# Attention and two expert layers on one core: 512-row groups in the second layer, 124-row blocks in the first

## Chip, cores and metric

The kernel runs on one core of a Trainium2 chip. The metric is the device time of one execution in microseconds. The profile shows one execution; "span" is the time from its first to its last instruction.

## What is computed

Attention with a block mask, then an expert layer that sends each of the 2304 tokens to two of eight experts, then one that sends each token to one of eight. Everything is in 32-bit floats. Cut from the reference:

```python
# q, k, v: 4 x 8 heads x 576 x 64; block mask of 64
scores = np.where(block_i >= block_j, scale * q @ k.T, -1e9)
x = softmax(scores) @ v                      # -> 2304 x 512
# first layer, w1: 8 x 512 x 1024, w2: 8 x 1024 x 512
noisy = x @ w_gate + np.log1p(np.exp(x @ w_noise)) * noise
top2 = the two largest of noisy, top2_w = their softmax
for e in range(8):
    h = np.maximum(x[mask] @ w1[e], 0.0)
    out[mask] += top2_w[mask, k, None] * (h @ w2[e])
# second layer, same shapes
logits = x @ w_gate2 + modality_bias[modality_id]
e_idx = argmax(logits); gate_w = softmax(logits)[e_idx]
out[mask] = gate_w[mask, None] * (np.maximum(x[mask] @ m2w1[e], 0.0) @ m2w2[e])
```

With these inputs the first layer's experts get 620, 582, 567, 546, 540, 559, 608 and 586 tokens. In the second layer experts 1 and 2 get 1165 and 1139 and the others none. Of the tokens that do not use expert 7 in the first layer, 866 and 852 go to these two.

## The kernel before

**Arithmetic.** Every 32-bit product is made of three matmuls in the faster 32-bit form: each operand is split into a high and a low part, and high x high, high x low and low x high are summed. For a weight piece of 128 x 1024, ScalarE copies `raw` to the high part `wh`, and VectorE or GpSimd subtracts to get the low part `wl` (`Stage.split`, L451). A job's weights are eight such pieces, fetched four ahead on SP's queue (`Stage.fetch`, L440).

**Jobs.** A `Job` (L466) is a set of rows for one expert. `gather` (L487) fetches its rows by index on GpSimd's queue into `xr`, `cols` (L499) transposes a block of 128 rows into PSUM `px` and splits it into `xth` (ScalarE) and `xtl` (VectorE). `mm1` (L511) is the first product, for each of eight column blocks of the hidden layer 12 matmuls over all rows of the job (in two halves where there are more than 512) into `ph`, evacuated to a high and a low part by ScalarE and VectorE (tiles `kp` and `hh`, `hl`). `mm2` (L527) is the second product, 24 matmuls of 512 columns for each block of 128 rows into `py`. The block's result `yr` is written by index: added to `X2` in the first layer, stored to the output in the second.

**Order of work.** The program is written out by a planner that keeps a clock for every engine (`clk`, L59) and emits each step when its estimated start is due; each engine then runs its instructions in the order written. `run` (L1407) goes through a list of jobs. During the second product of one job, `between` (L1428), called twice per block, puts in the transposes of the next job and the splits of its first four weight pieces; the other four are split during the first product, on the engines in the list `eb`.

**First layer.** Each expert has 640 places, five blocks of 128 (`CAP`, `NP`). Experts 0 and 1 begin with two and three blocks before attention has ended (`j00`, `j10`, tiles `ids0`), the rest of them follows (`j11`, `firsts[0]`), then experts 2 to 7. The routing runs in three steps (`route`, L650), for batches 0 and 1, batch 2, batch 3. Each turns the places of its tokens into lists: `hot_b` and `hot_a` make 0/1 operands `sl_ob`, `sl_oa` and `sl_ov`, and `lists` multiplies them on TensorE (`pt<-sl_ov,sl_ob`). `early` (L1135) makes from these the row numbers `idg` of a first job, which is gathered into the tile `wide`. Where more tokens choose an expert than it has places, a repair loop at the end of the program (L1593) runs.

**Notes.** For each finished block of the first layer eight dot products on VectorE (`zero<-py,gts,wide`) give the logits of the second layer, added by index to `LG`.

**Second layer.** `gates(k)` (L1466), the gate chain, reads `LG` back, picks each token's expert, counts with matmuls (`pt<-g_oh`), assigns tokens to groups of 256 rows, and makes the groups' lists in the same way. `gates(0)` starts after expert 6 and takes tokens that do not use expert 7: it fills three groups of 256 full rows (`NE`). `gates(1)` starts after expert 7 and fills seven (`NS`). The ten groups are jobs of two blocks (`group`, `job2`).

Of the kernel before, what the change touches and what calls it, by code (L numbers as in the profile page):

```python
# [7 lines left out]
F32 = mybir.dt.float32  # L8
# [22 lines left out]
def moe_kernel(tc, q, k, v, w_gate, w_noise, noise, w1, w2, mod_id, w_gate2, mod_bias, m2w1, m2w2, out):  # L31
# [6 lines left out]
    CAP = 640  # L38
    NP = CAP // 128

    FIRST = (2, 3)
    NE = 3
# [5 lines left out]
    NS = 10 - NE  # L48
# [55 lines left out]
    with ExitStack() as top:  # L104
# [18 lines left out]
        def iota(t, pattern, base=0, cm=0):  # L123
# [38 lines left out]
        table = [(cst.tile([128, 2 * n], I32, name="ids%d" % i), cst.tile([128, 2 * n], F32, name="gts%d" % i),  # L162
                  cst.tile([1, NG2 + 1], I32, name="eg%d" % i)) for i, n in ((2, NE), (3, NS), (4, NG2))]
# [25 lines left out]
        def consts2():  # L189
            iota(pad2, [[0, NA2]], base=NT + CAP, cm=1)  # L190
            iota(th2, [[G2, 9]])
            iota(th3, [[G2, 9]], base=G2 - 1)
            iota(th1, [[G2, 7]], base=CAP)
# [69 lines left out]
        def row_col(pool, pos, n):  # L263

            a = pool.tile([128, n], F32, name="sl_a%d" % n)
            bl = pool.tile([128, n], F32, name="sl_b%d" % n)
            vec.tensor_scalar(a, pos, 1.0 / 128, -63.5 / 128, op0=OP.mult, op1=OP.add)
            yield .3
            vec.tensor_scalar(a, a, 12582912.0, -12582912.0, op0=OP.add, op1=OP.add)
            yield .3  # L270
            vec.scalar_tensor_tensor(bl, a, -128.0, pos, op0=OP.mult, op1=OP.add)
            yield .3
            return a, bl
# [192 lines left out]
        class Job:  # L466


            def __init__(s, W, table, nt, ic, gc, emit, need=(None, None)):
# [29 lines left out]
            def cols(s, t, ps=None):  # L499
# [7 lines left out]
                cs = slice(128 * t, 128 * t + 128)  # L507
# [99 lines left out]
        def job1(e, t0=0, nt=NP, then=None, need=(None, None)):  # L607
            return Job((w1[e], w2[e]), X1, nt, lambda t: ids1[:, e * NP + t0 + t:e * NP + t0 + t + 1],
                       lambda t: gts1[:, e * NP + t0 + t:e * NP + t0 + t + 1], add_rows(ids1, e * NP + t0, nt, then), need)

        def group(W1, W2, table, ev, ic, gc, emit, need=(None, None)):
# [3 lines left out]
            return Job(w, table, G2 // 128, ic, gc, emit, need)  # L615
# [13 lines left out]
        def job2(k, g):  # L629
            ids, gts, eg = table[k]  # L630
            ic = lambda t: ids[:, 2 * g + t:2 * g + t + 1]
            j = group(m2w1, m2w2, X2, lambda: nc.sync.value_load(eg[0:1, g:g + 1], min_val=0, max_val=E - 1), ic,
                      lambda t: gts[:, 2 * g + t:2 * g + t + 1], put_rows(ic), ("eg%d" % k, "ids%d%d" % (k, g >= HG)))
# [12 lines left out]
        seconds = [job2(0, g) for g in range(NE)] + [job2(1, g) for g in range(NS)]  # L646
# [3 lines left out]
        def route(b0, nb):  # L650
# [81 lines left out]
            a, bl = yield from row_col(rt, pc.rearrange("p c k -> p (c k)"), 2 * C)  # L732
# [71 lines left out]
        with ExitStack() as ph:  # L804
# [330 lines left out]
            def early(e):  # L1135
# [11 lines left out]
                vec.tensor_scalar(base[:, e:e + 1], base[:, e:e + 1], 128.0 * n, None, op0=OP.max)  # L1147
# [259 lines left out]
        def run(jobs, hp_, ea, eb, nxt=None, stage=stage):  # L1407
# [3 lines left out]
            for n, j in enumerate(jobs):  # L1411
# [54 lines left out]
        def gates(k):  # L1466
# [4 lines left out]
            th = th2 if k else th3  # L1471
# [30 lines left out]
            n = yield from experts_of(pool, gn, gs, dst, "g_")  # L1502
            flags.add("eg%d" % k)
            if k == 1:

# [3 lines left out]
                no = yield from experts_of(pool, go, gso, eo, "o_")  # L1509
                m = pool.tile([1, 1], F32, name="g_m")  # L1510
                vec.tensor_scalar(m, n, -float(NS), 0.0, op0=OP.add, op1=OP.max)
                yield .3
                vec.tensor_add(m, m, no)
                yield .3
# [193 lines left out]
```

## Time and profile before

| | before |
|---|---|
| median of 3 runs | 992.0 us (990.72 to 994.84) |
| the profiled execution | 991.67 us |
| its span | 989.9 us |
| TensorE busy | 949.4 us (96%) |
| VectorE busy | 703.6 us (71%) |
| ScalarE, GpSimd busy | 520.9 and 521.0 us (53% each) |
| moved by DMA | 141.6 MB, mean 143 GB/s |
| mean granted TensorE clock | 0.993 of full speed |

Busy time is an average over stages. Attention runs up to about 268 us, the first layer to about 738 us, the second from there to the end. TensorE's matmuls overlap in the records, so the length of one matmul is not its price; the distance between starts is.

### The profile page before, as it was taken

What the parts mean: (1) busy time and instruction counts of PE and PEld (TensorE: products, weight loads), DVE (VectorE), ACT (ScalarE), POOL (GpSimd) and SP (SyncE); (2) the same over time, 40 slices, a digit from 0 to 9 for tenths busy, and PEclk for the clock granted to TensorE, in tenths of its full rate; (3) what the DMA queues carried; (4) which work ended last, traced back from release to release, by engine and by line L of the source; (5) the groups of instructions that cost most, each with busy time, mean ns of one, the idle gap of its engine ahead of it and who ended that gap; (6) DMA issues with size and microseconds to landing.
All of it is one profiled execution on the core that took longest, in us unless ns stands there. A gap on an engine that the chain in (4) does not pass through costs nothing.

```text
span 989.9 us, 17527 instructions
## 1 busy us (share of the span) xinstructions
PE 949.4 (96%) x6072; PEld 860.7 (87%) x6072; DVE 703.6 (71%) x1707; ACT 520.9 (53%) x1156; POOL 521.0 (53%) x488
## 2 busy tenths in 40 slices
PE   8999998999979999999999999999999899999995
PEld 6989897998868998989899898989979779999994
DVE  6878779888769967386693948669788866555450
ACT  6989997988542344334333333433335535555551
POOL 6234333464423599586685848648476253333321
PEclk9999999999989999999999999999999999999998
DMA  5577752222376377464563727434466877776620
GB/s 127 106 217 197 221 131 65 72 60 68 92 236 197 54 171 181 118 151 107 128 129 93 143 86 150 107 86 54 143 129 195 279 234 233 229 220 219 197 86 12
DMA packets 158258, 141.60 MB, mean 143 GB/s; under 512 B 76233, under 2 KB 124745, under 8 KB 158034
## 3 DMA queue, kind: packets, MB, share of 16 engines
q1 hardware_dynamic: 139042, 106.92, 37.4%
q0 software_dynamic: 18064, 33.23, 16.7%
q8 instruction: 50, 0.82, 0.3%
q14 instruction: 46, 0.38, 0.1%
q10 hardware_dynamic: 1056, 0.26, 0.1%
HBM read 112.54 MB, written 28.36 MB: 142 GB/s over the span
## 4 chain that ended last, share of the span: by engine, by line
PE 73%; DVE 9%; issue 5%; ACT 5%; DMA 4%; POOL 3%; SPq 1%; POOLq 0%; ACTq 0%; DVEq 0%
PE ph L71 28%; PE py L71 27%; PE pt L71 7%; PE ps L71 6%; PE pa L71 3%; PE px L71 2%; DVE wl L71 2%; ACT p L71 2%; POOL wl L71 2%; ACT kp L71 1%; DVE kp L71 1%; DMA xr<-X,ids 1%; DVE nm L71 1%; DVE PTl L71 1%; DMA qld<-in_q_dram 1%
## 5 line engine op out<-in xcount | busy, mean ns | idle before, releaser
L71 POOL TENSOR_TENSOR wl<-raw,wh 128x1024 fp32r<-128x1024 f32 x80 | 207.5, 2623 | 106.4 <-ACT wh L71 92.2
L71 PE MATMUL ph<-xth,wh 128*128 128x320 f32 (+2 forms) x800 | 241.2, 302 | 2.1 <-DVE kp L71 2.1
L71 PE MATMUL ph<-xth,wl 128*128 128x320 f32 (+2 forms) x800 | 240.0, 300 | 0.0
L71 PE MATMUL ph<-xtl,wh 128*128 128x320 f32 (+2 forms) x800 | 240.0, 300 | 0.0
L71 DVE SCALAR_TENSOR_TENSOR zero<-py,gts,wide 128x512 f32<-128x512 f32 x304 | 227.5, 748 | 8.3
L71 PE MATMUL py<-wh,kp 128*128 128x512 f32 x496 | 168.1, 399 | 0.0
L71 PEld LDWEIGHTS ph<-xth,wh 128*128 128x128 f32 x800 | 151.7, 190 | 4.0 <-DVE kp L71 2.8
L71 PEld LDWEIGHTS ph<-xtl,wh 128*128 128x128 f32 x800 | 151.7, 190 | 0.7
L71 PEld LDWEIGHTS ph<-xth,wl 128*128 128x128 f32 x800 | 151.7, 190 | 0.0
L71 ACT ACTIVATE wh<-raw 128x1024 fp32r<-128x1024 f32 x144 | 150.8, 1053 | 0.6 <-DMA raw<-in_moe_w_dram 0.5
L71 ACT ACTIVATE yr<-py,gts 128x512 f32<-128x512 f32 x60 | 41.3, 689 | 147.1 <-PE py L71 104.6
L71 PEld LDWEIGHTS py<-wh,kp 128*128 128x128 f32 x496 | 94.0, 189 | 18.5
L71 DVE SCALAR_TENSOR_TENSOR hl<-ph,hh 128x320 fp32r<-128x320 f32 (+2 forms) x100 | 46.4, 465 | 79.1 <-ACT hh L71 78.9
L71 DVE TENSOR_TENSOR wl<-raw,wh 128x1024 fp32r<-128x1024 f32 x64 | 80.1, 1259 | 29.8 <-ACT wh L71 29.1
L71 PE MATMUL py<-wl,kp 128*128 128x512 f32 x248 | 97.4, 393 | 0.0
L71 PE MATMUL ps<-kh,kp 128*128 128x256 f32 (+5 forms) x320 | 95.7, 340 | 0.6 <-ACT p L71 0.4
L71 POOL DMA_INDIRECT xr<-X,ids x55 | 57.5, 1045 | 73.5 <-PE px L71 44.2
L71 PE MATMUL py<-wh,hh 128*128 128x512 f32 x232 | 94.0, 405 | 0.0
L71 DVE TENSOR_TENSOR xtl<-px,xth 128x512 fp32r<-128x512 f32 x58 | 40.0, 690 | 74.3 <-ACT xth L71 74.3
L71 PE MATMUL py<-wl,hh 128*128 128x512 f32 x232 | 90.6, 390 | 1.7 <-POOL wl L71 1.7
L71 ACT ACTIVATE hh<-ph 128x320 fp32r<-128x320 f32 (+2 forms) x100 | 41.8, 418 | 95.1 <-PE ph L71 91.6
L71 PE MATMUL py<-wh,hl 128*128 128x512 f32 x232 | 90.9, 392 | 0.0
(253 smaller groups left out, 1830.9 us busy)
## 6 DMA issues: line engine op xcount, KB each, us to landing
raw<-in_moe_w_dram SPq DMA_DIRECT2D x144, 512.0 KB, 4.0
X<-zero SPq DMA_DIRECT2D x13, 512.0 KB, 4.2
kld<-in_k_dram SPq DMA_DIRECT2D x32, 128.0 KB, 2.9
vld<-in_v_dram SPq DMA_DIRECT2D x32, 128.0 KB, 2.7
X<-x SPq DMA_DIRECT2D x16, 256.0 KB, 2.6
qld<-in_q_dram SPq DMA_DIRECT2D x30, 128.0 KB, 2.8
wide<-in_moe_w_dram SPq DMA_DIRECT2D x4, 512.0 KB, 6.5
wide<-WG2T POOLq DMA_DIRECT2D x1, 2048.0 KB, 10.2
```

Source lines behind the costliest of these rows:

```text
L71: return f(*a, **kw)
```

## The change

**Second layer.** A group has 512 rows (`GW`), four blocks (`BW`). `gates(0)` fills two full groups, `gates(1)` two more full ones; what is left of each expert goes into two small groups, one of 256 rows and one of 128 (`job2(..., small=True)`, tile `egs`). In the group of 128 rows the first product reads its columns twice, so that each matmul has 256. With the inputs above this makes six groups out of ten: 512 rows of expert 1 and of expert 2, the same once more, then 141 tokens of expert 1 in 256 places and 115 of expert 2 in 128. `gates(1)` gets steps to assign the rest, and it now tells whether the repair loop must run by counting the placed tokens with one more matmul.

**First layer.** A block holds 124 tokens (`UNIT`), an expert 620 (`USED`). Neighbouring blocks overlap by four columns between the layers: the first product has 4 x 124 + 128 = 624 columns (two halves of 312) and the second reads blocks of 128 that begin at multiples of 124. The three-block job of expert 0 has 376 columns for 384. `j00`, `j10` and `j11` keep their steps of 128.

**Beside it.** In the second routing step `sl_ov` is made on VectorE instead of GpSimd (`b0 == 0`). For `firsts[0]` the four later weight pieces are split by GpSimd twice and then VectorE twice (`eb_`). The extra buffers for `raw` in the second layer are two instead of four.

```diff
+    UNIT = 124
+    USED = NP * UNIT
-    NE = 3
+    GW = 512
+    BW, NW, NSM = GW // 128, 2, 2
-    NS = 10 - NE
...
-        def row_col(pool, pos, n):
+        def row_col(pool, pos, n, u=128):
-            vec.tensor_scalar(a, pos, 1.0 / 128, -63.5 / 128, op0=OP.mult, op1=OP.add)
+            vec.tensor_scalar(a, pos, 1.0 / u, -(u - 1) / 2 / u, op0=OP.mult, op1=OP.add)
...
-                s.n = 128 * nt
+                s.n = step * (nt - 1) + 128
...
-                cs = slice(128 * t, 128 * t + 128)
+                cs = slice(s.step * t, s.step * t + (s.step if t < s.nt - 1 else 128))
+                pt = pt[:, :, 0:cs.stop - cs.start]
...
-                            ten.matmul(ph[:, 0:cn], w[:, kk], xx[:, kk, cs], start=(kk == 0 and i == 0), stop=(kk == 3 and i == 2))
+                            o, xx = ph[:, 0:cn], xx[:, kk, cs]
+                            if cn == 128:
+                                o, xx = ph[:, 0:2 * cn].rearrange("p (r c) -> p r c", r=2), bc(xx[:, None], [128, 2, cn])
+                            ten.matmul(o, w[:, kk], xx, start=(kk == 0 and i == 0), stop=(kk == 3 and i == 2))
...
-                cs = slice(128 * t, 128 * t + 128)
+                cs = slice(s.step * t, s.step * t + 128)
...
-        seconds = [job2(0, g) for g in range(NE)] + [job2(1, g) for g in range(NS)]
+        seconds = [job2(k, g) for k in range(2) for g in range(NW)] + [job2(1, g, True) for g in range(NSM)]
...
-                ov = yield from hot_a(rt, a[:, n], 10, 0, NA1, va[:, n], b0 + nb < B)
+                ov = yield from hot_a(rt, a[:, n], 10, 0, NA1, va[:, n], b0 == 0)
...
+                eb_ = [gps, gps, vec, vec] if j is firsts[0] else eb
-                        stage.split(eb[fs.index(f) % len(eb)] if "ids1" in flags else vec)
+                        stage.split(eb_[fs.index(f) % len(eb_)] if "ids1" in flags else vec)
...
             if k == 1:
+                nr = pool.tile([128, E], F32, name="g_nr")
+                vec.scalar_tensor_tensor(nr, gn, -float(GW), pp[:, NTT], op0=OP.mult, op1=OP.add)
+                gm, gr = yield from starts(pool, nr, th2, "q_")
+                yield from experts_of(pool, gm, gr, egs, "q_")
+                flags.add("egs")
...
+                    held = tl("held", dt=BF16)
+                    vec.tensor_copy(held, placed)
+                    pm = ps_r.tile([128, NTT], F32, name="pt")
+                    ten.matmul(pm, ones, held, start=True, stop=True)
+                    vec.tensor_reduce(m, pm[0:1], axis=AX, op=OP.add)
+                    vec.tensor_scalar(more, m, float(NT) - .5, None, op0=OP.is_lt)
...
-            with tc.tile_pool(name="ws2", bufs=4, reuse_waits="tile") as ws2:
-                rings["raw"].add(ws2, 4)
+            with tc.tile_pool(name="ws2", bufs=2, reuse_waits="tile") as ws2:
+                rings["raw"].add(ws2, 2)
```

**Where instructions move.** VectorE at the end of attention, before: the last weight halves and evacuation (`kp`) of the first job, then the routing's sum `acc` and the row numbers up to `idg`.

```order
L71 TENSOR_TENSOR wl<-qld,wh 128x512
L71 SCALAR_TENSOR_TENSOR kp_4115<-ps,kp_4115 128x256
L71 TENSOR_TENSOR acc_98<-acc_98,pt 128x200
L71 TENSOR_SCALAR si_u_4142<-acc_98 128x3
L71 SCALAR_TENSOR_TENSOR si_t_4141<-acc_98,pad_75 128x3
L71 SCALAR_TENSOR_TENSOR si_u_4142<-si_u_4142,acc_98 128x3
L71 TENSOR_TENSOR ids_101<-si_t_4141,si_u_4142 128x3
L71 TENSOR_TENSOR si_g_4147<-acc_98 128x3
L71 TENSOR_TENSOR gts_105<-si_g_4147,acc_98 128x3
L71 CAST i_4139<-ids_101 128x3
L71 TENSOR_SCALAR gp<-i_4139 128x3
L71 TENSOR_TENSOR idg_103<-gp,i_4139 128x3
```

VectorE at the same place after the change, from the list operands `sl_ov` on.

```order
L73 TENSOR_TENSOR sl_ov<-sl_oa,vals 128x1000 x2
L73 TENSOR_TENSOR wl<-kld,wh 128x512
L73 TENSOR_TENSOR wl<-qld,wh 128x512
L73 SCALAR_TENSOR_TENSOR kp_3955<-ps,kp_3955 128x256
L73 TENSOR_TENSOR acc_98<-acc_98,pt 128x200
L73 SCALAR_TENSOR_TENSOR kp_4039<-ps,kp_4039 128x256
L73 TENSOR_SCALAR si_u_4059<-acc_98 128x3
L73 SCALAR_TENSOR_TENSOR si_t_4058<-acc_98,pad_75 128x3
L73 SCALAR_TENSOR_TENSOR si_u_4059<-si_u_4059,acc_98 128x3
L73 TENSOR_TENSOR ids_101<-si_t_4058,si_u_4059 128x3
L73 TENSOR_TENSOR si_g_4064<-acc_98 128x3
L73 TENSOR_TENSOR gts_105<-si_g_4064,acc_98 128x3
```

`acc` stood behind all four pairs of weight halves and all eight evacuations; it now stands behind one pair and two evacuations. Between these rows and `idg` one more pair and one more evacuation follow. On TensorE the last seven of the ten list matmuls had all 96 matmuls of the first job's first product ahead of them; they now have 36 of them ahead and 60 behind.

TensorE at the start of the first group of the second layer, before: the last matmuls of expert 7's second product, then the group's first product.

```order
L71 MATMUL py<-wh,hh_8192 128x512
L71 MATMUL py<-wl,hh_8192 128x512
L71 MATMUL py<-wh,hl_8193 128x512
L71 MATMUL py<-wh,hh_8258 128x512
L71 MATMUL py<-wl,hh_8258 128x512
L71 MATMUL py<-wh,hl_8259 128x512
L71 MATMUL ph<-xth,wh 128x256
L71 MATMUL ph<-xtl,wh 128x256
L71 MATMUL ph<-xth,wl 128x256
```

TensorE at the same place after the change (`px` are the transposes of the group's rows).

```order
L73 MATMUL py<-wh,hh_8191 128x512
L73 MATMUL py<-wl,hh_8191 128x512
L73 MATMUL py<-wh,hl_8192 128x512
L73 MATMUL py<-wh,hh_8257 128x512
L73 MATMUL py<-wl,hh_8257 128x512
L73 MATMUL py<-wh,hl_8258 128x512
L73 MATMUL px<-ident,xr 128x128 x4
L73 MATMUL ph<-xth,wh 128x512
L73 MATMUL ph<-xtl,wh 128x512
L73 MATMUL ph<-xth,wl 128x512
```

The transposes of the fourth block stand immediately ahead of the first product, where twelve matmuls stood between them and the last transposes. Those of the second and third block stand twelve matmuls earlier, directly behind one another. One group later, the first transposes of the group whose rows `gates(1)` lists (`ids_110`) stand twelve matmuls behind the list matmuls, where they stood twenty-four behind.

## Rows read from the trace of the kernel before

**Rows 1.** The page, busy time of TensorE, with share of the span and instructions.
```profile
PE 949.4 (96%) x6072; PEld 860.7 (87%) x6072; DVE 703.6 (71%) x1707; ACT 520.9 (53%) x1156; POOL 521.0 (53%) x488
```
**Rows 2.** Waits of TensorE: line, waited for; us in total, times, longest.
```profile
PE px L71 <- DMA wide<-X,idg: 6.7, 1, 6.7
...
PE px L71 <- DMA xr<-X,ids: 3.1, 2, 1.9
PE ph L71 <- DVE kp L71: 2.1, 3, 1.1
PE py L71 <- POOL wl L71: 1.7, 1, 1.7
PE pt L71 <- DVE sl_ov L71: 1.6, 1, 1.6
```
**Rows 3.** Chain that ended last: start and length in us, what, instructions.
```profile
446.20 28.15 PE ph L71 x192
...
886.67 11.51 PE ph L71 x96
898.19 2.75 PE py L71 x12
901.37 2.77 PE py L71 x12
904.58 5.46 PE py L71 x24
```
**Rows 4.** Timeline, TensorE, 268 to 287 us: start, us, instruction, [idle before].
```profile
268.10 1.03 PE L71 MATMUL pt<-sl_ov,sl_ob 128*128 128x200 bf16 x10
...
278.58 1.11 PE L71 MATMUL px<-ident,wide 128*128 128x128 f32 x4 [6.67 <-DMA wide<-X,idg]
...
283.62 0.60 PE L71 MATMUL px<-ident,wide 128*128 128x128 f32 x4
...
286.82 0.60 PE L71 MATMUL px<-ident,wide 128*128 128x128 f32 x4
```
**Rows 5.** Timeline, GpSimd, 256 to 274 us.
```profile
256.34 4.42 POOL L71 TENSOR_TENSOR sl_ov<-sl_oa,vals 128x600 bf16<-128x600 bf16 x4
...
273.23 1.05 POOL L71 DMA_INDIRECT wide<-X,idg  x1 [9.78 <-DVE u L71]
```
**Rows 6.** Timeline, VectorE, 272 to 303 us.
```profile
272.31 0.16 DVE L71 TENSOR_TENSOR idg<-gp,i 128x3 int32<-128x3 f32 x1
...
302.33 1.20 DVE L71 TENSOR_TENSOR sl_ov<-sl_oa,vals 128x1000 bf16<-128x1000 bf16 x1
```
**Rows 7.** Stretches: busy PE, PEld, DVE, ACT, POOL; granted clock, DMA share, GB/s.
```profile
272.00:278.00 6.00, 0.00 (x0) 0.00 (x0) 1.46 (x8) 0.47 (x2) 2.95 (x3) 0.80 1.04 352
278.00:284.00 6.00, 5.42 (x21) 4.51 (x21) 3.10 (x9) 1.72 (x3) 0.00 (x0) 0.63 0.21 48
...
720.00:770.00 50.00, 47.04 (x296) 41.12 (x295) 44.42 (x107) 22.94 (x35) 34.35 (x22) 1.00 0.67 172
```
**Rows 8.** Timeline, GpSimd, 371 us: the late weight half of `firsts[0]`.
```profile
371.22 2.93 POOL L71 TENSOR_TENSOR wl<-raw,wh 128x1024 fp32r<-128x1024 f32 x1
```
**Rows 9.** Timeline, three engines, 726 to 733 us: the first group's rows.
```profile
726.58 1.02 POOL L71 DMA_INDIRECT xr<-X,ids  x1 [0.30 <-issue]
...
730.98 0.66 PE L71 MATMUL px<-ident,xr 128*128 128x128 f32 x4 [1.85 <-DMA xr<-X,ids]
...
731.47 0.95 POOL L71 DMA_INDIRECT xr<-X,ids  x1 [0.30 <-issue]
...
732.30 0.69 DVE L71 TENSOR_TENSOR xtl<-px,xth 128x512 fp32r<-128x512 f32 x1 [1.58 <-ACT xth L71]
```
**Rows 10.** Timeline, VectorE and TensorE, 803 to 810 us: the first late group's rows.
```profile
803.31 0.19 DVE L71 COPY g_acc<-pt 128x40 f32<-128x40 f32 x1
...
809.08 0.63 PE L71 MATMUL px<-ident,xr 128*128 128x128 f32 x4 [1.26 <-DMA xr<-X,ids]
```
**Rows 11.** The page, groups of instructions: busy us, mean ns of one, idle before.
```profile
L71 PEld LDWEIGHTS py<-wh,kp 128*128 128x128 f32 x496 | 94.0, 189 | 18.5
```

More of the change, by code (lines that the diff above doesn't have):

```diff
@@ L191, in consts2 @@
             iota(th2, [[G2, 9]])
-            iota(th3, [[G2, 9]], base=G2 - 1)
-            iota(th1, [[G2, 7]], base=CAP)
+            iota(th3, [[GW, 9]], base=GW - 1)
+            iota(th1, [[G2, 7]], base=USED)
             nc.sync.dma_start(wg2, w_gate2.rearrange("(k p) e -> p k e", p=128))
@@ L270, in row_col @@
             yield .3
-            vec.scalar_tensor_tensor(bl, a, -128.0, pos, op0=OP.mult, op1=OP.add)
+            vec.scalar_tensor_tensor(bl, a, -float(u), pos, op0=OP.mult, op1=OP.add)
             yield .3
@@ L466, in moe_kernel, with __init__ @@
         class Job:
-            def __init__(s, W, table, nt, ic, gc, emit, need=(None, None)):
+            def __init__(s, W, table, nt, ic, gc, emit, need=(None, None), step=128):
+                s.step = step
                 s.W, s.table, s.nt, s.ic, s.gc, s.emit, s.need = W, table, nt, ic, gc, emit, need
-                s.n = 128 * nt
+                s.n = step * (nt - 1) + 128
                 s.parts = [(0, s.n)] if s.n <= 512 else [(0, s.n // 2), (s.n // 2, s.n // 2)]
@@ L608, in job1, with group @@
             return Job((w1[e], w2[e]), X1, nt, lambda t: ids1[:, e * NP + t0 + t:e * NP + t0 + t + 1],
-                       lambda t: gts1[:, e * NP + t0 + t:e * NP + t0 + t + 1], add_rows(ids1, e * NP + t0, nt, then), need)
-        def group(W1, W2, table, ev, ic, gc, emit, need=(None, None)):
+                       lambda t: gts1[:, e * NP + t0 + t:e * NP + t0 + t + 1], add_rows(ids1, e * NP + t0, nt, then), need, 128 if nt == 2 else UNIT)
+        def group(W1, W2, table, ev, ic, gc, emit, need=(None, None), nt=G2 // 128):
             def w():
@@ L614, in w @@
                 return W1[bass.ds(e, 1)].rearrange("o d f -> (o d) f"), W2[bass.ds(e, 1)].rearrange("o f d -> (o f) d")
-            return Job(w, table, G2 // 128, ic, gc, emit, need)
+            return Job(w, table, nt, ic, gc, emit, need)
         prev_out = []
@@ L731, in route @@
             yield .3
-            a, bl = yield from row_col(rt, pc.rearrange("p c k -> p (c k)"), 2 * C)
+            a, bl = yield from row_col(rt, pc.rearrange("p c k -> p (c k)"), 2 * C, UNIT)
             big = rtile([128, 2 * C], "big")
@@ L1501, in gates @@
             gn, gs = yield from starts(pool, pp[:, NTT], th, "g_")
-            n = yield from experts_of(pool, gn, gs, dst, "g_")
+            yield from experts_of(pool, gn, gs, dst, "g_")
             flags.add("eg%d" % k)
             if k == 1:
+                nr = pool.tile([128, E], F32, name="g_nr")
+                vec.scalar_tensor_tensor(nr, gn, -float(GW), pp[:, NTT], op0=OP.mult, op1=OP.add)
+                yield .3
+                gm, gr = yield from starts(pool, nr, th2, "q_")
+                yield from experts_of(pool, gm, gr, egs, "q_")
+                flags.add("egs")
+                vec.tensor_scalar(gr, gr, 2.0, float(BW * NW), op0=OP.mult, op1=OP.add)
+                yield .3
+                vec.scalar_tensor_tensor(gr, gn, -float(BW), gr, op0=OP.mult, op1=OP.add)
+                yield .3
+                vec.tensor_add(nr, gs, gn)
+                yield .3
+                vec.tensor_scalar(nr, nr, NW + .5, 1e5, op0=OP.is_gt, op1=OP.mult)
+                yield .3
+                vec.tensor_add(gs, gs, nr)
+                yield .3
                 go, s_ = yield from starts(pool, base, th1, "o_")
@@ L1508, in gates @@
                 yield .3
[L1509 to L1514, printed above, removed]
-                vec.tensor_scalar(more, m, 1.0, None, op0=OP.min)
-                yield .3
+                yield from experts_of(pool, go, gso, eo, "o_")
             t0, pos, st = tl("t0", sh), tl("pos"), tl("st")
@@ L1602, in moe_kernel @@
             po = r1.tile(sh, F32, name="po")
-            vec.tensor_scalar(po, pos_k, float(CAP), 1e5, op0=OP.is_lt, op1=OP.mult)
-            vec.scalar_tensor_tensor(so, so, -float(CAP), po, op0=OP.add, op1=OP.add)
+            vec.tensor_scalar(po, pos_k, float(USED), 1e5, op0=OP.is_lt, op1=OP.mult)
+            vec.scalar_tensor_tensor(so, so, -float(USED), po, op0=OP.add, op1=OP.add)
             vec.tensor_copy(ovs.rearrange("p c k -> p k c"), so)
```

48 lines of the change are left out of this document (35 added, 13 removed).

## The prediction

> **What bounds the kernel now.** I read the busy times first: TensorE is busy for 949 us of the span [rows 1], far ahead of the others, so what counts is the time its instructions take and the moments when it stands still. The list of waits comes next [rows 2]: TensorE loses 6.7 us in one wait for a gather into `wide`, 3.1 us in two waits for gathered rows (1.85 and 1.26 us), 2.1 us in three for the evacuation `kp`, 1.7 us in one for a low weight half `wl` made on GpSimd, 1.6 us for `sl_ov`. The list has no others in the two layers' products. Then the chain of work that ended last [rows 3], which in these stretches is TensorE alone, gives the price of every matmul from one start to the next: 28.15 / 192 = 0.1466 us at 320 columns, 11.51 / 96 = 0.1199 at 256, 5.46 / 24 = 0.2275 at 512. From 256 to 512 columns that is 0.42 ns per column on top of a fixed 12 ns per matmul. Four transposes into `px` add 901.37 - 898.19 - 12 x 0.2275 = 0.45 us.
>
> **The change, part by part.** All sums are made against the profiled execution's own 991.67 us; the median of the runs, 992.0, is 0.3 above it.
>
> *Second layer, arithmetic.* I ran the reference on its inputs: only two experts are chosen in the second layer, 1165 and 1139 tokens. So ten groups of 256 rows become two groups of 512 early, two of 512 late, one of 256 and one of 128. First product: 960 matmuls x 0.1199 = 115.1 us before. Now 4 x 96 x 0.2275 = 87.4, plus 2 x 96 x 0.1199 = 23.0 (the 128-row group computes its columns twice, as 256): 110.4. Gain 4.7 us. Nothing in the trace has 512 columns in the first product; I take the price of the second product, which has the same number of columns and one weight load per matmul as well. Second product: 19 blocks instead of 20, 24 x 0.2275 = 5.5 us, and one set of transposes, 0.45. Sum 10.6 us, all of it on the path, since TensorE does not wait in these groups [rows 3].
>
> The Trainium skill (TensorE: Matmul & The Clock Gate, "Wait — 56ns, not 53.3ns?") gives a fixed cost of about 2.5 ns per matmul. By that, 384 matmuls fewer would save 1.0 us in the first product. The trace shows 12 ns [rows 3] and decides.
>
> *First layer, columns.* Six experts have 2 x 96 matmuls each with 312 columns for 320: 1152 x 8 x 0.42 ns = 3.9 us. The three-block part of expert 0 goes from 384 to 376: 0.3 us. Sum 4.2, on the path. The second product there still has 128 rows a block.
>
> *Weights.* 32 of 144 weight pieces are no longer loaded and split. TensorE hardly waits for them, so I count nothing for it; the cover is that a 512-row group lasts about 45 us where 256 rows last 23.4 [rows 3] for the same eight pieces. The 128-row group has the least cover, some 17 us, but its pieces are fetched ahead. Half the extra buffers in that phase (two for four) I also put at nothing.
>
> *End of attention.* Before, the list operands `sl_ov` of the second routing step are made on GpSimd in four operations, 4.42 us [rows 5], and the list matmuls stand behind all first-product matmuls of the first job, at 268.10 [rows 4]. The row numbers `idg` follow at 272.31 [rows 6], the gather is issued at 273.23 [rows 5], and TensorE, idle since 271.9, goes on at 278.58 [rows 4]. Now `sl_ov` takes two VectorE operations of 1.20 us [rows 6], in a stretch where VectorE waits for ScalarE between weight halves, and 60 matmuls that were ahead of the last list matmuls stand behind them: 60 x 0.12 = 7.2 us earlier. In VectorE's order two weight halves and two `kp` now stand between `acc` and `idg`, which gives back 1 to 2 us. So the gather starts 5.2 to 6.2 us earlier, at 267.0 to 268.0. It took 5.35 us [rows 4, 5] under full DMA load (352 GB/s in 272 to 278, [rows 7]); another took 4.4 us [rows 9]. It lands between 271.4 and 273.4, and TensorE asks at 271.9. I leave 0.5 us of the wait.
>
> After the wait the granted clock was 0.63 on average in 278 to 284, against 1.00 in 720 to 770 [rows 7], so part of the stretch ran at 1.2 GHz: transposes and 12 matmuls took 283.62 - 278.58 = 5.04 us where the next such set took 3.20 [rows 4]. These 1.84 us go with the wait. Gain 6.67 - 0.5 + 1.84 = 8.0 us. Next late there is nothing TensorE asks for: the weights of the second job were loading from 268 on.
>
> *Expert 0, rest.* TensorE waits 1.7 us [rows 2] for a `wl` that GpSimd made from 371.22 on, behind other work [rows 8]. Two of these four halves go to VectorE, which stands idle between evacuations there. Gain 1.7 us.
>
> *From the first layer to the second.* This part speaks against the change. Four blocks must be gathered and transposed where two were.
> - The first gather still makes TensorE wait about 1.85 us [rows 9].
> - Gathers follow each other by about 1.3 us on GpSimd; the third, issued at about 731.5, takes 4.4 like the first and lands near 735.9, while its transposes now stand directly behind the second block's, at about 735.0: 0.9 us.
> - The fourth block's transposes now stand immediately ahead of the first product. From the start of transposes to the end of `xtl` it is 732.30 + 0.69 - 730.98 = 2.0 us [rows 9], of which TensorE works 0.4: 1.6 us new.
> - The first late group's gather: its transposes wait until 809.08, 5.8 us after `acc` at 803.31 [rows 10], about 6.9 after the list matmuls. Between those and the transposes stood 24 matmuls, now 12 (2.7 us). The wait of 1.26 becomes 3.1 to 4.1; I take 3.5.
> - The other four waits of this stretch (`kp` twice, `g_oh`, `sl_ov`; 3.8 us in all, [rows 2] holds the sums) stem from the second gate chain, which gets some twenty short VectorE steps more (4 to 5 us), but about 9 us more of TensorE work to hide behind. Between 0 and 3.8; I take half, 1.9.
>
> Before: 1.85 + 1.26 + 3.8 = 6.9. After: 1.85 + 0.9 + 1.6 + 3.5 + 1.9 = 9.75. Loss 2.8 us. The tail behind the last matmul is unchanged.
>
> **Sum.** 10.6 + 4.2 + 8.0 + 1.7 - 2.8 = 21.7. 991.67 - 21.7 = 970.0; with the 0.3 up to the median, 970.3 us.
>
> **Rivals.**
> 1. *The passage to the second layer costs more.* The gate chain runs late in spite of the longer groups (3.8 instead of 1.9), the gather wait is 4.1, and one or two of the idle stretches bring the clock down. For it: the long idle stretch at 272 did so and cost 1.84 us; against it: 720 to 770, with 1.85 us of idle at 730.98, was granted 1.00 [rows 7, 9]. 970.3 + 1.9 + 0.6 + 2 x 1.84 = 976.5.
> The Trainium skill (the same page, "Why this matters for your kernels") warns that gaps between bursts of matmuls bring TensorE back to the low clock; that speaks for this rival, and rows 7 show it once.
> 2. *The longer groups hide the gate chain completely* and the fourth block costs little: 970.3 - 1.9 - 0.9 - 0.5 = 967.0.
> 3. *The gather at the end of attention stays late*, since the weight loads saturate the DMA at just that time: only 4 of the 8 us are won, 974.3.
> 4. *A first product at 512 columns costs just twice one at 256*: 4 x 96 x 2 x 0.1199 = 92.1 in place of 87.4 us, 4.7 less gain, 975.0. For it: no row has this form; against it: the prices at 256, 320 and 512 lie on one line [rows 3].
> The Trainium skill's 2.5 ns, named above, comes close to this case.
> 5. *Slower: weight loads from odd offsets.* Hidden blocks of the first layer now begin at multiples of 496 bytes and not 512. A weight load of 189 ns hides under a matmul of 227 [rows 3, 11]. Should the odd start cost it, 26 blocks x 24 loads are hit, and the gain is gone once a load takes more than 227 + 21.7 us / 624 = 262 ns; doubled (378 ns), it is 0.15 x 624 = 94 us, some 1064 us. Against it: the list matmuls read their moving operand in steps of 400 bytes, and ten of 200 columns took 1.03 us with their end [rows 4], no more than their columns need; for weights no row shows it.
> 6. *The change does not hold its rows.* By the reference the fullest first-layer expert has exactly 620 rows, and 5 x 124 = 620. One more, and the repair loop runs: at least one group of 23.4 us [rows 3] with nothing beside it, so 993.7 or more.
>
> **How the numbers follow.** Forecast 0.53, rival 1 0.17, rival 2 0.12, rivals 3 and 4 0.07 and 0.06, rivals 5 and 6 0.03 and 0.02. The forecast's own spread is about 4 us either way (the second-layer waits between their bounds, the gather between 0 and 1.5 us late). The range from 964.5 to 977 takes in rivals 1 to 4 and leaves out the two slow ones and mixtures of several misfortunes. About 0.5% is what a measurement of this kernel can tell from no change, 987 to 997 us: only a large part of rival 1, 3 and 5 together would end there, 0.02. Slower 0.04, faster 0.94.
>
> **What would show it.** After the change, the wait for the gather into `wide` should be under 1.5 us and the granted clock there 1.0; a 312-column expert should take 27.5 us in the first product and a 512-row one 21.8; the wait for `wl` near 365 us should be gone; and the waits on gathered rows should add up to some 6 us in place of 3.1, the largest ahead of the first late group, with a wait of `ph` on `xtl` new. Wrong would be: weight loads well over 189 ns in the first layer, a second or longer wait at the end of attention, or a gate chain that makes TensorE wait for more than 4 us.

## The result, and the profile after

The changed kernel takes 983.2 us (median of four runs, 979.6 to 984.6), 0.989 of the kernel before with a 95% interval of 0.985 to 0.993. It is faster, as forecast, but by 9 us and not by 22; 970.3 us and the range up to 977 were wrong. The profiled execution, the longest of the four, took 984.6 us with a span of 982.8, so 7.1 us less than the profiled execution before. Ratios here and below are of runs that agree with one another; one run of the later kernel `e6_small`, of 3482.4 us and without a trace to explain it, is in none of them.

The page of the changed kernel, line of busy times (against [rows 1]), and then TensorE's waits from 262 us on: line, waited for; us in total, times, longest (against [rows 2]).

```profile
PE 943.6 (96%) x5661; PEld 835.6 (85%) x5661; DVE 681.4 (69%) x1676; ACT 482.6 (49%) x1090; POOL 489.6 (50%) x472
```
```profile
PE px L73 <- DMA xr<-X,ids: 4.5, 3, 2.8
PE px L73 <- DVE xtl L73: 3.1, 2, 1.7
PE pt L73 <- DVE sl_ov L73: 2.7, 1, 2.7
PE pt L73 <- DVE g_held L73: 2.5, 1, 2.5
PE ph L73 <- DVE kp L73: 1.2, 2, 0.9
PE ph L73 <- ACT xth L73: 0.9, 1, 0.9
```

The wait for the gather into `wide` (6.7 us) and the one for `wl` (1.7) are gone. Three kinds of wait are new: for `xtl`, for `xth` and for `g_held`; the one for `sl_ov` is longer.

The granted clock changed too. Stretches of the changed kernel: us, busy PE, PEld, DVE, ACT, POOL, then granted clock, DMA share, GB/s.

```profile
668.00:700.00 32.00, 32.00 (x228) 31.30 (x227) 24.98 (x81) 12.32 (x23) 16.06 (x9) 1.00 0.24 46
705.00:710.00 5.00, 2.30 (x10) 1.23 (x8) 4.93 (x6) 0.00 (x0) 3.03 (x2) 0.86 0.79 177
710.00:715.00 5.00, 5.00 (x24) 4.10 (x24) 4.93 (x12) 0.69 (x1) 1.25 (x1) 0.80 0.22 84
730.00:735.00 5.00, 3.59 (x14) 2.85 (x13) 2.87 (x8) 1.20 (x2) 4.09 (x4) 0.74 0.58 105
795.00:800.00 5.00, 4.01 (x13) 3.24 (x14) 2.62 (x11) 0.33 (x1) 0.00 (x0) 0.73 0.35 105
820.00:825.00 5.00, 4.05 (x13) 3.35 (x14) 2.22 (x4) 1.54 (x2) 3.95 (x4) 0.66 0.71 228
825.00:932.00 107.00, 107.00 (x506) 87.90 (x505) 36.97 (x49) 38.42 (x54) 25.93 (x21) 1.00 0.43 135
```

Before, the clock stood at 1.00 in 720 to 770 us [rows 7]. Now four stretches lie between the levels of 1.2 and 2.4 GHz, each at or just behind an idle stretch of TensorE: 2.70 us of idle up to 708.5 (two rows, 705 to 715), 3.1 us in three pieces between 724 and 731.5, 2.51 us up to 796, 2.80 us up to 820.9. In the last one seven matmuls of 512 columns take 824.64 - 821.54 = 3.10 us where they take 1.6 at full clock.

The chain of the work that ended last: start and length in us, what, instructions; an expert of the first layer, then a 512-row group (against [rows 3]).

```profile
437.71 27.68 PE ph L73 x192
...
468.58 2.79 PE py L73 x12
...
481.45 13.93 PE py L73 x60
```
```profile
841.96 21.76 PE ph L73 x96
863.72 2.72 PE py L73 x12
...
876.50 10.91 PE py L73 x48
```

The 512-column first product costs 21.76 / 96 = 0.2267 us, as forecast. The first layer's second product is slower than before: 60 matmuls take 13.93 us, where they took 13.62. The row of the kernel before:

```profile
432.58 13.62 PE py L71 x60
```

Where the time went, by starts of matmuls in the two timelines (the last line runs to the end of the span); the forecast is the prediction's own, split at the same places (two more sets of transposes are counted ahead of group 0):

| From .. to | Before, us | After, us | Gain | Forecast |
|---|---|---|---|---|
| First second-product matmul (268.9) .. expert 2's first product | 119.38 | 110.97 | 8.4 | 10.0 |
| .. expert 7's first product | 288.80 | 288.27 | 0.5 | 3.2 |
| .. group 0's first product ("passage") | 60.49 | 69.67 | -9.2 | -2.8 |
| .. end | 252.32 | 244.95 | 7.4 | 11.2 |

### The profile page after: what moved, and what is told of

Read it like the earlier page. It is cut to its first block, busy times and chain, and to the rows that moved or that the text cites. A ratio compares the mean times of both kernels' runs of the same rounds, so it can differ in the third digit from the quotient of the medians.

```text
span 982.8 us, 16351 instructions
## 1 busy us (share of the span) xinstructions
PE 943.6 (96%) x5661; PEld 835.6 (85%) x5661; DVE 681.4 (69%) x1676; ACT 482.6 (49%) x1090; POOL 489.6 (50%) x472
## 4 chain that ended last, share of the span: by engine, by line
PE 70%; issue 11%; DVE 6%; POOL 5%; ACT 4%; DMA 3%; SPq 0%; POOLq 0%; ACTq 0%; DVEq 0%
PE py L73 25%; PE ph L73 25%; PE pt L73 8%; PE ps L73 6%; PE pa L73 3%; POOL wl L73 2%; PE px L73 2%; ACT p L73 2%; DMA raw<-in_moe_w_dram 1%; DVE wl L73 1%; DMA xr<-X,ids 1%; DVE PTl L73 1%; ACT kp L73 1%; DMA qld<-in_q_dram 1%; POOL out_dram L73 1%
## 5 line engine op out<-in xcount | busy, mean ns | idle before, releaser
L73 POOL TENSOR_TENSOR wl<-raw,wh 128x1024 fp32r<-128x1024 f32 x70 | 180.9, 2602 | 113.8 <-ACT wh L73 111.2
L73 PE MATMUL ph<-xth,wh 128*128 128x312 f32 (+4 forms) x672 | 217.2, 323 | 2.1 <-DVE kp L73 1.2
L73 PE MATMUL ph<-xtl,wh 128*128 128x312 f32 (+4 forms) x672 | 216.9, 323 | 0.2 <-DVE xtl L73 0.2
L73 PE MATMUL ph<-xth,wl 128*128 128x312 f32 (+4 forms) x672 | 217.1, 323 | 0.0
L73 PEld LDWEIGHTS ph<-xth,wl 128*128 128x128 f32 x672 | 126.9, 189 | 5.2
L73 ACT ACTIVATE wh<-raw 128x1024 fp32r<-128x1024 f32 x112 | 117.8, 1052 | 2.1 <-DMA raw<-in_moe_w_dram 2.1
L73 DVE SCALAR_TENSOR_TENSOR hl<-ph,hh 128x312 fp32r<-128x312 f32 (+5 forms) x84 | 43.0, 514 | 78.8 <-ACT hh L73 78.7
L73 ACT ACTIVATE hh<-ph 128x312 fp32r<-128x312 f32 (+5 forms) x84 | 38.4, 457 | 99.8 <-PE ph L73 99.6
L73 DVE TENSOR_TENSOR xtl<-px,xth 128x512 fp32r<-128x512 f32 (+1 forms) x57 | 38.9, 682 | 64.6 <-ACT xth L73 64.6
L73 ACT ACTIVATE kp<-ph 128x312 fp32r<-128x312 f32 (+5 forms) x84 | 38.4, 457 | 91.8 <-PE ph L73 91.4
```

Source lines behind the costliest of these rows:

```text
L73: return f(*a, **kw)
```

## Experiments

The lengths below are taken between the same places; "late part" is the last row of the table. Each is from one profiled execution, and kernels that were not edited at a place differ there too: 110.3 to 111.0 us in the first row of the table, 67.95 to 72.32 in the passage, 241.6 to 245.0 in the late part. A smaller difference shows nothing by itself.

**The 512-row groups alone.** The blocks of 124 rows, the move of `sl_ov` and the split of expert 0's halves are undone; the two extra buffers stay:

```diff
-    UNIT = 124
+    UNIT = 128
-                ov = yield from hot_a(rt, a[:, n], 10, 0, NA1, va[:, n], b0 == 0)
+                ov = yield from hot_a(rt, a[:, n], 10, 0, NA1, va[:, n], b0 + nb < B)
-                eb_ = [gps, gps, vec, vec] if j is firsts[0] else eb
+                eb_ = eb
```

> The 512-row groups alone: the changed kernel with blocks of 128 rows and 640 columns in the first layer, with sl_ov of the second routing step made on GpSimd and with the four weight halves of expert 0's rest on GpSimd, as before the change. By the parts of the two traces (from expert 7's first product to the end 302.1 us of records before and 303.6 after) the groups give back in the passages all that they save: 990 to 995 us, 0.998 to 1.002 of the kernel before, with an expert at 57.75 us as before. By the prediction's own sum they would bring 10.6 - 2.8 = 7.8 us, 0.992.

Measured: 989.8 us, 0.9967 of before (0.9955 to 0.9979), between the two expectations. The passage takes 69.53 us (9.0 more than before), the late part 242.22 (10.1 less). So the arithmetic is worth about what was forecast, and the passage gives most of it back.

**The other two parts, each undone by itself**: the move of `sl_ov`, and the split of expert 0's weight halves.

> The changed kernel with the list operand sl_ov of the second routing step made on GpSimd again, as before the change. If the gain at the end of attention stems from this move, as the prediction says, the wait for the gather into wide comes back (6 to 7 us at about 278), the clock behind it falls below 0.8, and expert 2's first product starts 7 to 8 us later than 379.91, at about 387. Rival (the gain stems from the three-block part or the weights): less than 3 us are lost.

> The changed kernel with all four weight halves of expert 0's rest made on GpSimd, as before the change. By the prediction the wait for wl at about 365 comes back and expert 2's first product starts 1.7 us later against the first second-product matmul at 268.94 (110.97 in the changed kernel, 112.7 here). Rival (the wait went with the end of attention, which moved everything ahead of it): 111.0 stays.

Measured, from 268.9's place to expert 2's first product (110.97 in the changed kernel): 118.22 us with `sl_ov` on GpSimd and 112.45 with the halves there. Both waits are back, the first one's only 0.6 us shorter than in [rows 4]. Timeline of TensorE, `e7_slov` and `e14_eb`: start, us, instruction, [idle before].

```profile
280.10 1.11 PE L73 MATMUL px<-ident,wide 128*128 128x128 f32 x4 [6.09 <-DMA wide<-X,idg]
```
```profile
369.23 0.50 PE L73 MATMUL py<-wl,hh 128*128 128x512 f32 x1 [1.74 <-POOL wl L73]
```

These two parts bring 7.2 and some 1.5 us, about what the whole change gains.

**The bank of the transposes.**

```diff
-                            nx.cols(left[0])
+                            nx.cols(left[0], ps_h if left[0] % 2 else None)
```

> The changed kernel with every second block's transposes written to a PSUM bank of the hidden products' pool, so that they need not wait until the block before has been read out. Theory B (one PSUM bank for the transposes is what holds TensorE up where blocks follow each other closely): the waits for xtl at 279.91 (1.68 us) and 731.55 (1.41 us) go, the stretch at the low clock behind the second one is shorter, and the passage from expert 7's first product to group 0's takes 3 us less than 69.51, about 66.5. Rival (the transposes wait for gathered rows anyway, and the bank only hides it): the waits carry another name, and less than 1 us is won.

Measured: 976.4 us in one run beside 990.8 of the kernel before; passage 62.57. TensorE's timeline at the second and third block, changed kernel and `e2_px2`:

```profile
729.51 0.63 PE L73 MATMUL px<-ident,xr 128*128 128x128 f32 x4 [0.27 <-DMA xr<-X,ids]
731.55 0.66 PE L73 MATMUL px<-ident,xr 128*128 128x128 f32 x4 [1.41 <-DVE xtl L73]
```
```profile
725.55 0.66 PE L73 MATMUL ph<-ident,xr 128*128 128x128 f32 x4 [0.43 <-DMA xr<-X,ids]
726.63 0.63 PE L73 MATMUL px<-ident,xr 128*128 128x128 f32 x4 [0.43 <-DMA xr<-X,ids]
```

The 1.41 us become 0.43, and the clock stays at 1.00 in 720 to 740. At the end of attention the rival was right: the wait for `xtl` (1.68 us) turns into one for `m` of 1.69, and the 0.4 us won are within what kernels without the edit differ by. The passage is shorter by more than this edit explains, because the wait for `sl_ov` is missing as well; in `e5_both` below, where it is back, the passage is 65.72, some 4 us less than in the changed kernel. Why it is missing is seen next.

**VectorE and GpSimd at `sl_ov`.** Group 0's weight halves made on VectorE instead of GpSimd:

```diff
-                            stage.split(ea[left[1] % len(ea)] if "ids1" in flags else vec)
+                            stage.split(vec if nx is seconds[0] or "ids1" not in flags else ea[left[1] % len(ea)])
```

> The changed kernel with the low weight halves of group 0 made on VectorE instead of GpSimd while expert 7 runs its second product. Theory D (the list operand sl_ov took 4.02 instead of 0.53 us because GpSimd worked on wl at the same time): sl_ov takes 0.5 us, the wait of 2.70 us at 708.49 and the low clock behind it go, the passage is 3 to 4 us shorter than 69.51. Rival (VectorE is simply too full there): sl_ov is short but comes later behind four splits of 1.2 us, and the wait stays over 2 us.

Measured: `sl_ov` takes 0.53 us and its wait is gone, as in theory D. But the passage is no shorter, 71.50 us: TensorE now waits 4.36 us for VectorE to read a bank of the second product, and 2.57 for gathered rows. The rival was right that VectorE is too full, though the loss sits at another place than it said.

The timelines show what happened. VectorE and GpSimd, changed kernel:

```profile
700.63 2.38 DVE L73 TENSOR_TENSOR vals<-g_t,vals 128x18 bf16<-128x18 f32 x1
702.89 1.35 DVE L73 TENSOR_TENSOR sl_ob<-lane,sl_b 128x1152 bf16<-128x1152 f32 x1
704.16 0.22 DVE L73 TENSOR_TENSOR sl_oa<-lane,sl_a 128x72 bf16<-128x72 f32 x1
704.41 4.02 DVE L73 TENSOR_TENSOR sl_ov<-sl_oa,vals 128x360 bf16<-128x360 bf16 x1
```
```profile
700.53 2.40 POOL L73 TENSOR_TENSOR wl<-raw,wh 128x1024 fp32r<-128x1024 f32 x1 [7.55 <-ACT wh L73]
703.41 2.26 POOL L73 DMA_INDIRECT X<-yr,ids  x1 [0.48 <-ACT yr L73]
705.13 2.90 POOL L73 TENSOR_TENSOR wl<-raw,wh 128x1024 fp32r<-128x1024 f32 x1
```

And in `e2_px2`, where `sl_ob` starts together with `wl`:

```profile
701.32 1.35 DVE L73 TENSOR_TENSOR sl_ob<-lane,sl_b 128x1152 bf16<-128x1152 f32 x1
702.59 2.44 DVE L73 TENSOR_TENSOR sl_oa<-lane,sl_a 128x72 bf16<-128x72 f32 x1
705.06 0.60 DVE L73 TENSOR_TENSOR sl_ov<-sl_oa,vals 128x360 bf16<-128x360 bf16 x1
```
```profile
701.32 3.62 POOL L73 TENSOR_TENSOR wl<-raw,wh 128x1024 fp32r<-128x1024 f32 x1 [7.74 <-ACT wh L73]
```

In the changed kernel `vals` (0.21 us elsewhere) ends when the first `wl` ends, and `sl_ov` (0.53 elsewhere) shortly after the second. In `e2_px2` `sl_ob` is not delayed and `wl` is, by 1.2 us; then `sl_oa` waits for the end of `wl`. One stands still until the other is done, and here a shift of 0.1 us went with a change of the loser. What is not explained is the start of `sl_ov`: by its usual length it would have ended 0.2 us ahead of the record of the second `wl`. The indirect DMA that GpSimd issues at that time is not enough to hold it: in `e4_vecsplit` one runs from 702.72 to 704.29, and `sl_ov`, started at 702.90, takes 0.53 us. Evacuations such as `zero` (0.75 us beside `wl` in both kernels) are not touched; they read one of their two operands from PSUM.

The Trainium skill (SBUF — State Buffer, "Who interferes with whom") states that a VectorE instruction with two SBUF inputs contends with a GpSimd instruction that reads SBUF, that the port pair they share is "an exclusive lock", and that the order of issue decides who blocks. The rows above agree. The expectations for `e4_vecsplit` and `e6_small` speak of VectorE steps with bf16 output; that is not the condition, since `sl_a` with f32 output is held up below.

The kernel before had such steps too, at the same place (VectorE, then GpSimd):

```profile
709.85 2.35 DVE L71 CAST vals<-g_t 128x18 bf16<-128x18 f32 x1
...
713.84 0.44 DVE L71 TENSOR_TENSOR sl_ov<-sl_oa,vals 128x270 bf16<-128x270 bf16 x1
```
```profile
709.76 2.39 POOL L71 TENSOR_TENSOR wl<-raw,wh 128x1024 fp32r<-128x1024 f32 x1 [7.51 <-ACT wh L71]
...
714.58 2.96 POOL L71 TENSOR_TENSOR wl<-raw,wh 128x1024 fp32r<-128x1024 f32 x1
```

One step was held for the length of a `wl`, a cast with a single input, and TensorE did not wait for the chain there. `sl_ov` ended 0.3 us ahead of the next `wl`; it went free by that margin. The prediction did not read these rows.

**The count of placed tokens.** The five steps from `held` to `more`, with their matmul, moved from the middle of `gates(1)` to its end:

```diff
                 if k:
                     vec.tensor_add(placed, placed, new)
                     yield .3
-                    held = tl("held", dt=BF16)
-                    ...
-                    vec.tensor_scalar(more, m, float(NT) - .5, None, op0=OP.is_lt)
-                    yield .3
...
+            if k == 1:
+                held = tl("held", dt=BF16)
+                ...
             flags.discard("chain")
```

> The changed kernel with the count of placed tokens (the copy g_held, its matmul and the two steps behind it) moved to the end of the second gate chain, behind the lists. Theory C (the round trip through TensorE in the middle of the chain costs its wait and the clock behind it): the wait for g_held (2.51 us) goes, the clock in 795 to 800 us is 1.0 instead of 0.73, the lists come about 3 us earlier, the late gather's wait (2.80 us) shrinks, and group 0's start to the end takes 3 to 6 us less than 244.95. Rival (the chain is late as a whole): the 2.5 us come back as a wait for sl_ov.

Measured: 977.8 us in one run beside 990.8 of the kernel before; late part 239.4, which is 5.5 less than in the changed kernel and 2.2 less than the shortest without this edit. The three kernels under "Together" have the edit as well, and their late parts are 239.0 to 239.4. The late gather's wait shrinks to 1.61 us and the clock is 1.00 in 795 to 800 and in 815 to 825; 1.87 us come back as waits for `sl_ov`. The wait of theory C is gone, with a part of the rival.

But the round trip was not late by itself. In the changed kernel a step of the same chain, ahead of the count, is held up by GpSimd (VectorE, then GpSimd):

```profile
792.50 2.32 DVE L73 TENSOR_TENSOR sl_a<-sl_a,g_msk 128x18 f32<-128x18 f32 x1
```
```profile
792.42 2.36 POOL L73 TENSOR_TENSOR wl<-raw,wh 128x1024 fp32r<-128x1024 f32 x1 [5.13 <-ACT wh L73]
```

In the first chain `sl_a` takes 0.18 us. By these rows some 2.1 of the 2.51 us that TensorE waits for `g_held` are the same loss as at `sl_ov`. The edit takes away the matmul that waits, not the hold: in `e3_held` `sl_a` still takes 2.36 us. Cutting these later halves into pieces was not tried.

**The clock by itself.** Ten matmuls of ones without use in two of the idle stretches:

```diff
+        def busy():
+            ph = ps_h.tile([128, 512], F32, name="ph")
+            for _ in range(10):
+                ten.matmul(ph.rearrange("p (r c) -> p r c", r=4), ones, bc(ones[:, None, :], [128, 4, 128]), start=True, stop=True)
```

> The changed kernel with ten matmuls of ones without use (512 columns, about 2.2 us at full clock) in TensorE's order ahead of the first list matmuls of the early groups (the wait of 2.70 us at 708.49) and ten ahead of the first late group's transposes (the wait of 2.80 us at 820.95). Theory E (the idle stretch itself brings the clock down, and the slow matmuls behind it cost 1.2 to 1.7 us more): the granted clock in the 5 us behind both places is 1.0 instead of 0.80 and 0.66, the list matmuls and the transposes start where they did, and the matmuls behind them take 0.23 us from the first on; 1.2 and 1.7 us less in these places, the second of which goes to the end. Rival (the clock falls for another reason, such as many short matmuls): it falls here too.

Stretches of `e13_busy`, columns as above:

```profile
705.00:710.00 5.00, 4.37 (x28) 2.25 (x26) 4.96 (x4) 0.00 (x0) 3.44 (x2) 1.00 0.74 180
710.00:715.00 5.00, 5.00 (x33) 3.79 (x30) 4.86 (x12) 0.69 (x1) 1.88 (x1) 1.00 0.26 99
...
820.00:825.00 5.00, 5.00 (x29) 3.24 (x28) 0.19 (x1) 0.69 (x1) 3.78 (x5) 1.00 0.82 258
825.00:830.00 5.00, 5.00 (x31) 4.01 (x29) 3.58 (x5) 1.55 (x2) 1.92 (x2) 1.00 0.63 218
```

The clock stays at 1.00 in both places. The seven second-product matmuls behind each take 1.97 us with the lists between them (3.48 in the changed kernel) and 1.70 us (3.10). So an idle stretch there costs 1.4 to 1.5 us on top of itself. In the whole this does not show: the late part is 0.9 us shorter, within the differences between traces, the wait for `g_held` grows to 2.94, and one run gave 982.4 us beside 992.3 of the kernel before.

**The first layer.** Hidden blocks from aligned columns; then, besides, the tiles as wide as before:

```diff
-                cs = slice(s.step * t, s.step * t + 128)
+                o = min(128 * t, s.n - 128)
+                cs = slice(o, o + 128)
```
```diff
-                return [pool.tile([128, n], F32R, name="h%s%d" % (x, f)) for x in "hl"]
+                return [pool.tile([128, 640 if n == 624 else n], F32R, name="h%s%d" % (x, f))[:, 0:n] for x in "hl"]
```

(the same for `xth` and `xtl`).

> The changed kernel, but the second product of the first layer takes its hidden blocks from columns 0, 128, 256, 384 and 496 (of the three-block part 0, 128 and 248) instead of multiples of 124, so that nearly all weight loads start at multiples of 64 bytes; the rows of the result are therefore mixed up, the work is the same. Theory A (the start of the weight load costs): 60 matmuls of 512 columns take 13.62 us as before the change and not 13.92, an expert 57.0 instead of 57.64 us, and expert 7's first product starts some 3 us earlier against expert 2's. Rival (the 0.3 us come from something else, such as the DMA traffic or the evacuations): the 13.92 us stay.

> e1_aligned (hidden blocks at columns 0, 128, 256, 384, 496) and besides the tiles of hidden values and of transposed rows made 640 columns wide, of which 624 are used, so that every tile starts where it did with 640; again the rows of the result are mixed up and the work is the same. Theory A2 (the place in SBUF costs, through the start of the tiles): the second product of an expert with its transposes takes 29.63 us as before the change instead of 29.97, the first product 27.5 instead of 27.68. Rival (the place does not matter): 29.9 and 27.68 stay.

Per expert (mean of four), first product and then second product with transposes: before 28.15 and 29.61, after 27.68 and 29.98, `e1_aligned` 27.68 and 29.92, `e10_pad` 27.50 and 29.69. Theory A fell: the blocks' starts alone bring 0.06 us. Theory A2 holds: with the tiles in their old places as well, the first product costs what the line through [rows 3] gave, and the second nearly what it cost before. The halves of the hidden values bear this out: `kp` lies in tiles of 640 columns in every kernel, `hh` and `hl` do not. Mean distance between starts of second-product matmuls, `kp` and then `hh` with `hl`, in ns: before 231.8 and 233.2, after 233.8 and 236.3, aligned blocks 232.2 and 236.9, wide tiles alone (`e11_best`, below) 233.3 and 235.0, both 231.9 and 233.3. Aligned blocks alone help where the tile is wide already. Timeline of TensorE in `e10_pad`: first matmul of a first product, of the second product, and of the next expert.

```profile
438.06 0.30 PE L73 MATMUL ph<-xth,wh 128*128 128x312 f32 x1
...
465.56 0.40 PE L73 MATMUL py<-wh,kp 128*128 128x512 f32 x1
...
495.26 0.30 PE L73 MATMUL ph<-xth,wh 128*128 128x312 f32 x1
```

**Together.** The second bank and the moved count; then also group 0's weight halves on GpSimd in four pieces (`k = cut or ...` in `split`, with `cut` 256); then also the wide tiles, with blocks at multiples of 124 as in the change.

> The changed kernel with both edits that won time: the second PSUM bank for the transposes (as in e2_px2) and the count of placed tokens at the end of the chain (as in e3_held). Theory B + C (the two losses are separate): the passage from expert 7's to group 0's first product takes some 62 to 64 us, group 0's start to the end 227 us, and the whole 969 to 972 us, 0.978 of the kernel before. Rival (both edits recover the same time, since the gate chains are late anyway): about 976, like the better one alone.

> e5_both with the low weight halves of group 0 made on GpSimd in four pieces of 256 columns instead of one of 1024. Theory D (a VectorE step with bf16 output stands still until the running GpSimd subtraction is done): no vals, sl_oa or sl_ov step there takes more than 1.2 us (0.2 to 0.6 us of its own and at most one piece of 0.6 to 0.7), where in the kernels so far one or two took 2.3 to 4.0; whether the time falls depends on who loses in e5_both, 0 to 2 us less. Rival (GpSimd's work does not hold VectorE up; sl_ov waits for something else): a step over 2 us stays.

> e6_small with the tiles of hidden values and of transposed rows of the five-block jobs made 640 columns wide, of which 624 are used; the blocks still begin at multiples of 124, and the whole result is computed. Theory A3 (where the tiles start is what matters, the blocks' own start little): an expert takes 57.2 to 57.3 us instead of 57.65, 2 to 3 us less in all, some 970.5 us by the median or 0.9745 of the kernel before. Rival (both matter together, as the two steps of e1_aligned and e10_pad might mean): an expert takes 57.5 or more and the time stays that of e6_small.

| Kernel | us, median | Ratio to before, 95% interval | Passage | Late part |
|---|---|---|---|---|
| `e5_both` | 977.3 | 0.9827 (0.9809 to 0.9845) | 65.72 | 239.0 |
| `e6_small` | 972.5 (of three) | 0.9772 (0.9749 to 0.9796) | 63.16 | 239.2 |
| `e11_best` | 970.5 | 0.9778 (0.9765 to 0.9791) | 63.15 | 239.4 |

`e5_both` is slower than expected: `sl_ov` takes 4.02 us there again and TensorE waits 2.61 for it. Its profiled run was the best of four (974.3; the others 977.1 to 977.6). The rival's 976 is nearer than the 969 to 972 of theory B + C; the 227 us expected for the late part do not fit that sum either. In `e6_small` GpSimd's pieces let VectorE in between (VectorE first, then GpSimd):

```profile
702.11 0.64 DVE L73 TENSOR_TENSOR vals<-g_t,vals 128x18 bf16<-128x18 f32 x1
...
704.71 0.97 DVE L73 TENSOR_TENSOR sl_ov<-sl_oa,vals 128x360 bf16<-128x360 bf16 x1
```
```profile
701.95 4.33 POOL L73 TENSOR_TENSOR wl<-raw,wh 128x256 fp32r<-128x256 f32 x4 [7.50 <-ACT wh L73]
```

The wait is gone, and the interval lies below that of `e5_both`. (`sl_ob` took 2.59 us once, 709.45 on, beside GpSimd's next work; no wait of TensorE names it.) In `e11_best` the first product is at 27.50 us, the second at 29.87, an expert at 57.37: between theory A3 and its rival. The first product needs the wide tiles, the second these and the blocks' starts. The ratios of the last two do not differ; in the trace the first layer is 1.4 us shorter over five experts. By their ratios both beat the changed kernel and the one before.

## Why the prediction was right in sign and wrong in size

**Right.** The second layer's arithmetic: 21.76 us against 21.8, blocks at 5.5 us, and the last two groups as foretold. The end of attention: the gather no longer holds TensorE up, the clock there is 1.00, and undoing the move costs 7.2 us where 8.0 stood; what remains is a wait of 1.68 us for `xtl`, behind routing steps and a weight half in VectorE's order, where 0.5 were left for the gather. The wait for `wl`: 1.5 for 1.7.

**The step that failed: "From the first layer to the second", 9.75 us after the change against 6.9 before.** The same stretch now holds 12.5 us of waits (700 to 825 us) and some 6.4 us of slow matmuls behind them: 1.5, 1.65, 1.6 and 1.7 us in the four low stretches. That is 18.9 us, a loss of 12 and not of 2.8. In its parts:
- First gather, 1.85 foretold, 1.45 measured; fourth block 1.6 and 1.1; late gather 3.5 and 2.8. These were sized well.
- Third block: 0.9 foretold for a late gather; 0.27 + 1.41 measured, most of it for the one PSUM bank of the transposes. That two blocks directly behind one another share a bank was not in the sum, though the order of instructions showed them side by side.
- "The other four waits ... I take half, 1.9": the longer groups did hide the evacuation waits, but `sl_ov` of the first chain moved to where GpSimd was working on `wl` (2.70 us). In [rows 2] all waits of this kind together were 1.6. The sum has no price for VectorE and GpSimd holding each other up.
- The round trip for `g_held` (2.51 us) was not priced. The diff adds a matmul in the middle of the chain, and TensorE, in order, stands at it until VectorE has got there; GpSimd's `wl` held VectorE up for 2.1 us just ahead of it. With `sl_ov` that is more than the 4 us of waiting for a gate chain which the prediction named as a sign of being wrong.
- The clock: rival 1 had one or two low stretches with a chance of 0.17; there were four. Its evidence against, 1.85 us of idle at full clock [rows 9], holds: 1.45 and 1.68 us alone left the clock at 1.00 here too. But the forecast itself put 3.5 us into one place, and 6.67 had brought the clock down [rows 7].

**The second term that was mis-sized: first layer, columns, 4.2 us.** It measured 0.5 us over five experts. Rival 5 looked at the right place for the wrong cost: the weight loads still take 188 to 190 ns, but matmuls got slower by 1 to 3 ns each, from the width of the tiles and the starts of the blocks.

The sum of the three misses is 9.2 us in the passages, some 3.3 in the first layer and 1.6 at the end of attention, 14.1 of the 14.6 us between 21.7 and 7.1. Rival 1, at 976.5, was nearest.

## What to carry to other kernels

Making groups larger saves matmuls but lines up what smaller groups interleave: look in the new order for blocks that share one PSUM bank, for a matmul that waits in the middle of a VectorE chain, and for VectorE steps with two SBUF inputs beside GpSimd work, and price each. The last kind shows in the trace of before as a short VectorE step that takes as long as the GpSimd step beside it, even where nobody waits for it yet. The waits of 2.5 to 2.8 us here cost another 1.5 us or so each at the low clock, which belongs into the price too. When a tile shrinks by a few columns, keep its old width in SBUF and measure again.

## What the runs showed of the hardware

- GpSimd's subtraction over 1024 columns holds a VectorE step with two SBUF operands up for up to its whole length: 2.38 for 0.21 us, 2.32 for 0.18, and 4.02 for 0.53 (part of this last one stays open, see above). A cast with one input was held too, 2.35 us. It can be the other way round, 3.62 for 2.40 us. In four pieces the longest of these steps ahead of the list matmuls was 0.97 us.
- How wide tiles are laid out in SBUF, and so where they and their parts start, changes the speed of matmuls that read them: 27.68 against 27.50 us for 192 matmuls of 312 columns, with rows of 2496 and 2560 bytes per partition. The weight loads' own times did not change. The Trainium skill (SBUF — State Buffer, "Operand start alignment") asks only for multiples of the element size and says that this is about legality, not speed; these runs show a price within that rule. Which multiple matters was not tried; steps that are multiples of 64 bytes were not enough (2496 is 39 x 64, and the aligned blocks start at multiples of 64 in their tile).
- Ten matmuls without use, put into idle stretches after which the clock had fallen, kept it at its upper level (1.00 instead of 0.66 and 0.80).
